# Weight steps put behind the float32 heads' exponentials, the first 24 feed-forward units ordered block by block, and other buffers for w_out

## The chip, the cores and the metric

The kernel runs on one core of one Trainium2 chip. The metric is the device time of one execution in microseconds (us). Matrix products run on the tensor engine (PE, its weight loads as PEld), activations and copies with a scale on the scalar engine (ACT), element-wise work on the vector engine (DVE), masks and reductions across partitions on GpSimd (POOL); the sync engine (SP) issues most DMAs, ACT those of the weights. Every engine takes its own queue in order.

## The reference

All inputs are float64. Attention over 8 batches of 8 heads with 576 positions and 64 channels, with a causal mask and a bias from a running sum of a gate `s`, is followed by a gated feed-forward layer over all 4608 tokens (512 channels, 1536 hidden).

```python
scores = scale * np.matmul(q, k.transpose(0, 1, 3, 2))
cum = np.cumsum(np.maximum(s, 0.0), axis=-1)
bias = -(cum[:, :, :, None] - cum[:, :, None, :])
scores = np.where(causal, -1000000000.0, scores + np.minimum(bias, 0.0))
attn = np.exp(scores - scores.max(-1, keepdims=True)); attn /= attn.sum(-1, keepdims=True) + 1e-09
x = np.matmul(attn, v).transpose(0, 2, 1, 3).reshape(B * S, H * D)
return ((1.0 / (1.0 + np.exp(-(x @ w_gate)))) * (x @ w_val) @ w_out).astype(np.float32)
```

## The kernel before

Operands are split into a high and a low float16 part, and three products of parts stand for one exact product. There are four kinds of work.

**Float32 heads.** Heads 0 to 7 (batch 0) are computed with float32 matmuls, tile by tile (five row tiles a head): scores on PE (L575), mask on POOL (L461), bias and row minimum on DVE (L584, tile `em`), exponential on ACT (L587), transposes on PE (L596), copies on ACT (L597), products with v on PE (L605).

**Float16 heads.** Heads 8 to 63 use the split operands (scores L446 and L447, minimum L471, exponential L474, splits L478, L483, L491, DMA transposes, products L506 to L511).

**Weight steps.** The weights arrive as 64-bit floats and are decoded on the chip. There are 18 steps (`wsteps`): steps 0 to 11 hold one block of 128 hidden columns of w_gate and w_val, steps 12 to 17 two such blocks of w_out. A step loads 1 MB in two DMAs issued by ACT (L253, L260), then runs as a chain across engines: ACT L272 (128x1024), DVE L273, L274, L275, ACT L287 (sum of squares), POOL L289, DVE L125 and L127 (a power of two as scale), ACT L292 (high part), DVE L293 (low part). Its raw words lie in a "room": `raw0`, or a quarter of the not yet written `w2all`, or a part of `t2big`, which later holds results of the first 24 units. Decoded words lie in `dec0` (tile `wa`) or in `w2all`; all six w_out steps use `dec0`, one after the other. `room(n)` also gives the step that must be through before the load of step n may be issued.

**Feed-forward units.** A unit (g, f) is 256 tokens times one block f of the hidden columns: 24 matmuls for gate and value (`ffn_in`, L657, tile `gv`), tanh on ACT (L662), the product on DVE (L664, tile `t2`). Then the two halves of h are made (`ffn_mid`, ACT L672 and DVE L673), and w_out is applied (`ffn_out`, L687, tile `o`, 6 matmuls with 512 columns). The scale of h (`hidden_scale`, tile `hsc`) needs the scales of all 18 weight steps. So the 24 units of the first two token groups (g = 0 and 1), whose x is ready after head 7, keep their t2 in `t2big` until step 17 is through; from g = 2 on, h follows at once.

The program is written as ticks, five to a head, and a list scheduler reorders the instructions of each engine when the kernel is built, by its own estimate of when each is ready; `tc.high_priority` and `tc.keep_in_program_order` constrain it, and the queue of each engine is then fixed. Weight steps are written at ticks below 44 (`min(2 + n // 8, 6)`: six of them) and, from tick 44 on, ahead of the units that need them: before unit 0, 3, 6, 9 the next three blocks, before unit 8 the first w_out step, from unit 12 all the others. Loads of steps 12 and 13 are written at ticks 22 and 30.

Of the kernel before, what the change touches and what calls it, by code (L numbers as in the profile page):

```python
# [23 lines left out]
def tile_attention_then_gated_ffn(  # L24
# [198 lines left out]
    for i in (1, 2):  # L223
        raw.append(t2big[:, 8 * i * GT : 8 * (i + 1) * GT].bitcast(I32).rearrange("p (n t) -> p n t", t=2))
    outroom = [(4, 0, 0), (5, 0, 0), (0, 0, NF - 3), (3, 0, NF - 1), (5, 0, NF + 1), (0, 0, NF + 2)]
# [9 lines left out]
    def load_weight(n):  # L235
# [3 lines left out]
        for x, src in enumerate((w_out,) if o else (w_gate, w_val)):  # L239
# [6 lines left out]
            if o == 0:  # L246
                src = src.rearrange("(c p) n -> p c n", p=P)
                dst = dst.rearrange("p (c x n) -> p c x n", c=NC, x=2)[:, :, x]
            else:

                src = src.rearrange("(x p) (h n) -> x p h n", p=P, h=8)
                dst = dst.rearrange("p (h x n) -> x p h n", x=2, h=8)
                ins = nc.scalar.dma_start(dst[0], src[0])  # L253
                if n < NF + 2:
                    tc.keep_in_program_order(ins)
                src, dst = src[1], dst[1]
            if n < 2:
                nc.sync.dma_start(dst, src)
            else:
                ins = nc.scalar.dma_start(dst, src)  # L260
                if n == 2 or NF <= n < NF + 2:
                    tc.keep_in_program_order(ins)

    def decode_weight(n):
# [7 lines left out]
        nc.scalar.activation(a.bitcast(F32), r[:, :, 1].bitcast(F32), AF.Copy, scale=2.0 ** -112)  # L272
# [45 lines left out]
    wnext = {"load": 0, "step": 0}  # L318

    def weight_step():  # L320
        n = wnext["step"]
        while n and wnext["load"] < len(wsteps) and room(wnext["load"])[2] < n:
            if not NF <= wnext["load"] < NF + 2:
                load_weight(wnext["load"])
# [253 lines left out]
    def n_max(i, t):  # L578
# [8 lines left out]
        nc.scalar.activation(e_t[t][:m, :w], e_t[t][:m, :w], AF.Exp, bias=init, scale=-1.0)  # L587
# [60 lines left out]
    def ffn_in(g, f):  # L648
# [14 lines left out]
        t2 = t2first[g * NF + f] if g < 2 else fp.tile([P, GT], F32, tag="t2", name=f"t2_{g}_{f}")  # L663
# [46 lines left out]
    units = [(g, f) for g in range(NG) for f in range(NF)]  # L710
# [9 lines left out]
    def emit_out():  # L720
        if state["o"] < len(units):
            ffn_out(*units[state["o"]])
# [15 lines left out]
    OUT = (22, 30)  # L738
    WLA = 3
    nticks = NTL * NH  # L740
    for n in range(nticks + 12):
# [43 lines left out]
        if i < NH:  # L785
# [96 lines left out]
            if n in OUT:  # L882
                load_weight(NF + OUT.index(n))
# [36 lines left out]
    for tt in range(GT // P):  # L920
        for u in range(state["o"], len(units)):
            ffn_out(*units[u], tiles=(tt,), last=True)
# [28 lines left out]
```

## Time and profile before

| | |
|---|---|
| time, median of 3 runs | 1153.24 us (1152.33 to 1156.69) |
| span of the profiled execution | 1146.4 us; its own time is not listed apart, the three runs are 5.9 to 10.3 us above the span |
| PE, busy | 1091.6 us (95%) |
| DVE, ACT, POOL, busy | 776.1, 749.5, 261.3 us |
| granted tensor clock, mean | 0.985 |
| the float32 heads | until 111.6 us (last exponential of head 7) |
| last weight step (low part, L293) | starts at 182.4 us |
| first w_out matmul | 189.0 us |

The span divides in two. From about 267 us on PE is busy nearly without a break. Ahead of that, float32 heads, weight steps, float16 heads 8 to 17 and the first 24 units share the engines, and PE waits now and then. Busy time counts overlapping instructions once. A matmul's record is longer than its pitch (a w_out matmul: record 0.379 us, one every 0.216 us), so a busy PE can be less than full.

### The profile page before, as it was taken

The numbers are of one execution on the slowest core, as the hardware profiler recorded it, in microseconds if no ns is written. First come the engines' busy times: TensorE is split into PE (matmuls) and PEld (weight loads), VectorE is DVE, ScalarE is ACT, GpSimd is POOL, SyncE is SP. The second block draws the span as 40 slices with busy tenths as digits, with TensorE's granted clock in tenths as the row PEclk, the third lists the DMA queues.
The fourth block names the chain that finished last, engine by engine and source line by source line (L and its number), as shares of the span: only waits on it lengthen the run. The fifth ranks groups of instructions, "written<-read, shape, count | busy, mean of one in ns | idle before, by whom it ended". The sixth has DMA issues, their size and how long they took to land.

```text
span 1146.4 us, 30336 instructions
## 1 busy us (share of the span) xinstructions
PE 1091.6 (95%) x11644; PEld 853.5 (74%) x11644; DVE 776.1 (68%) x2395; ACT 749.5 (65%) x1465; POOL 261.3 (23%) x568
## 2 busy tenths in 40 slices
PE   6787888989999999999999999999999999999998
PEld 4566676658767887788777777778877887787775
DVE  6899999866787777776565677777777775222222
ACT  6989778667777777676665577767776764233222
POOL 6634233222232222121211122212222221000000
PEclk9889899999999999999999999999999999999999
DMA  9676868995989888777646498868887774000000
GB/s 280 201 217 161 185 139 181 183 189 130 171 164 175 164 178 167 141 150 138 145 79 139 89 178 166 166 144 171 156 161 138 150 124 88 13 20 20 1 19 19
DMA packets 445518, 157.62 MB, mean 137 GB/s; under 512 B 403583, under 2 KB 435839, under 8 KB 445374
## 3 DMA queue, kind: packets, MB, share of 16 engines
q1 hardware_dynamic: 418686, 127.38, 57.6%
q10 hardware_dynamic: 23328, 17.04, 4.9%
q0 software_dynamic: 3360, 11.27, 3.0%
q8 instruction: 91, 1.49, 0.5%
q14 instruction: 53, 0.43, 0.1%
HBM read 56.92 MB, written 9.58 MB: 58 GB/s over the span
## 4 chain that ended last, share of the span: by engine, by line
PE 76%; DMA 7%; DVE 5%; issue 5%; ACT 5%; SPq 1%; POOL 1%; ACTq 0%; DVEq 0%; POOLq 0%
PE gv L657 42%; PE o L687 22%; PE s L447 3%; PE s L446 3%; DMA qk<-in_q_dram 1%; PE av L506 1%; PE av L508 1%; PE av L507 1%; DMA v<-in_v_dram 1%; DVE e L471 1%; PE s L575 1%; DMA pt<-p 1%; DMA T<-T 1%; PE na_ps L605 1%; DMA nqk<-in_q_dram 1%
## 5 line engine op out<-in xcount | busy, mean ns | idle before, releaser
L657 PE MATMUL gv<-x,w 128*128 128x256 f16 (+3 forms) x6912 | 613.2, 246 | 5.3 <-DVE t2f L664 2.7
L657 PEld LDWEIGHTS <-w 128*128 128x128 f16 x6912 | 533.8, 98 | 61.5 <-issue 5.2
L687 PE MATMUL o<-w2all,h 128*128 128x512 f16 x1296 | 314.8, 379 | 0.0
L461 POOL TENSOR_SCALAR_AFFINE_SELECT rl<-rl 128x64 f32<-128x64 f32 (+1 forms) x280 | 111.5, 399 | 519.7 <-DVE em L471 465.3
L474 ACT ACTIVATE e<-e,em 128x576 f32<-128x576 f32 x280 | 154.6, 554 | 92.3 <-DVE em L471 90.2
L687 PEld LDWEIGHTS <-h 128*128 128x128 f16 x1296 | 123.6, 98 | 108.7 <-issue 2.4
L662 ACT ACTIVATE th<-gv,scb 128x256 f32<-128x256 f32 (+3 forms) x288 | 111.4, 412 | 139.3 <-PE gv L657 138.4
L664 DVE SCALAR_TENSOR_TENSOR t<-th,gv 128x256 f32<-128x256 f32 x192 | 80.2, 417 | 133.5 <-ACT th L662 132.5
L471 DVE CUSTOM_DVE_ANT_0 e<-s,rl,qkcf 128x288 f32<-128x288 f32 x280 | 135.8, 485 | 30.5 <-PE s L447 24.9
L672 ACT ACTIVATE h<-t,hsc 128x256 f16<-128x256 f32 x192 | 96.6, 503 | 80.0 <-DVE t L664 80.0
L483 DVE SCALAR_TENSOR_TENSOR p<-e,p 128x384 f16<-128x384 f32 x224 | 102.0, 495 | 40.2 <-ACT p L478 39.4
L673 DVE SCALAR_TENSOR_TENSOR h<-t,hsc,h 128x256 f16<-128x256 f32 x192 | 93.2, 486 | 43.3 <-ACT h L672 42.8
L478 ACT ACTIVATE p<-e 128x1152 f16<-128x1152 f32 x112 | 112.1, 1001 | 2.8
L506 PE MATMUL av<-v,pt 128*128 128x65 f16 x560 | 68.0, 193 | 6.9 <-DMA pt<-p 6.9
L507 PE MATMUL av<-v,pt 128*128 128x64 f16 x560 | 68.0, 192 | 0.0
L446 PE MATMUL s<-T 128*128 128x288 f16 (+2 forms) x246 | 64.6, 280 | 3.6 <-DMA T<-qk 2.6
L508 PE MATMUL av<-v,pt 128*128 128x65 f16 x560 | 67.9, 194 | 0.0
L447 PE MATMUL s<-T 128*128 128x288 f16 (+2 forms) x246 | 62.2, 282 | 2.4 <-DMA T<-T 2.4
L506 PEld LDWEIGHTS <-pt 128*128 128x128 f16 x560 | 52.4, 97 | 13.6 <-DMA pt<-p 8.8
L706 POOL DMA_DIRECT2D out_dram<-osb x34 | 19.4, 570 | 174.6 <-ACT osb L705 173.8
L409 POOL PARTITION_BROADCAST cr<-cr x63 | 57.5, 913 | 6.1 <-DVE em L584 5.7
L455 DVE TENSOR_SCALAR rl<-cr,qkcf 128x576 f32<-128x576 f32 x56 | 29.1, 520 | 40.1 <-POOL cr L409 39.9
(157 smaller groups left out, 1436.9 us busy)
## 6 DMA issues: line engine op xcount, KB each, us to landing
v<-v SPq DMA_DIRECT2D x56, 162.5 KB
out_dram<-osb POOLq DMA_DIRECT2D x34, 256.0 KB, 2.9
v<-in_v_dram SPq DMA_DIRECT2D x64, 128.0 KB
T<-T SPq DMA_DIRECT2D x82, 72.0 KB
t2f<-in_v_dram SPq DMA_DIRECT2D x20, 288.0 KB
qk<-in_q_dram SPq DMA_DIRECT2D x17, 288.0 KB
qk<-in_k_dram SPq DMA_DIRECT2D x17, 288.0 KB
w2all<-in_moe_w_gate_dram ACTq DMA_DIRECT2D x7, 512.0 KB
```

What stands on the lines that cost most here:

```text
L446: nc.tensor.matmul(ps[:, : b_ - a], lhs, T[i][:, 0, a:b_], start=True, stop=False)
L447: nc.tensor.matmul(ps[:, : b_ - a], lhs, T[i][:, 2, a:b_], start=False, stop=True)
L461: nc.gpsimd.affine_select(rl[i][:, q0:w], rl[i][:, q0:w], pattern=[[-1, m]], compare_op=ALU.is_ge, fill=-MASKED if i < NN else MASKED, bas ...
L471: nc.vector.tensor_tensor_reduce(e_t[t][:, a:b_], ps[:, : b_ - a], rl[i][:, a:b_], c, init, ALU.add, ALU.min, acc)
L474: nc.scalar.activation(e_t[t][:, :w], e_t[t][:, :w], AF.Exp, bias=init, scale=-1.0)
L478: nc.scalar.activation(p_s[h_][:, 0], e_s[h_], AF.Copy, scale=PSCALE)
L483: nc.vector.scalar_tensor_tensor(flat[:, LOW[t] * P : (LOW[t] + t) * P], e_t[t][:, : t * P], PSCALE, flat[:, kb * P : (kb + t) * P], ALU.m ...
L506: nc.tensor.matmul(AV[i][:, t], hi, v_[:, D : 2 * D + 1], start=kb == 0, stop=False)
L657: nc.tensor.matmul(ps[:, gv, a:e], w1[f][:, cc, gv, wl], x_of(b, cc)[:, xl, c0 + a : c0 + e], start=(c == 0), stop=(c == 3 * NC - 1))
L662: nc.scalar.activation(th[:, a:e], ps[:, 0, a:e], AF.Tanh, scale=scb[b][:, f : f + 1])
L672: nc.scalar.activation(h[:, 0], t2, AF.Copy, scale=hsc[:, f : f + 1])
L687: nc.tensor.matmul(ps[:m], h[:, hl, tt * P : tt * P + m], w2[f][:, wl], start=(f == 0 and c == 0), stop=(f == NF - 1 and c == 2))
```

## The change

Four edits. The decode's first instruction (L272) is queued on ACT behind the exponential of a float32 head that was written last (`tc.issue_after`; it sets the order and waits for nothing). Seven steps in place of six are written below tick 44. The first 24 units are written block by block, (0,0), (1,0), (0,1), (1,1) and so on, in place of group by group, and the steps from 7 on are tied to blocks: three ahead each third block, step 12 from block 8 on, steps 13 to 17 at block 11. And the rooms of w_out change: only step 12 keeps a part of `t2big` as early room, the others reuse `raw0` and `w2all` once earlier steps have left them, so that loads 13 to 15 may be issued after step 11, load 16 after step 14, load 17 after step 16.

```diff
-    for i in (1, 2):
-        raw.append(t2big[:, 8 * i * GT : 8 * (i + 1) * GT].bitcast(I32)...)
-    outroom = [(4, 0, 0), (5, 0, 0), (0, 0, NF - 3), (3, 0, NF - 1), (5, 0, NF + 1), (0, 0, NF + 2)]
+    raw.append(t2big[:, 16 * GT : 24 * GT].bitcast(I32)...)
+    outroom = [(4, 0, 0), (2, 0, NF - 1), (0, 0, NF - 3), (3, 0, NF - 1), (0, 0, NF + 2), (0, 0, NF + 4)]
...
-        nc.scalar.activation(a.bitcast(F32), r[:, :, 1].bitcast(F32), AF.Copy, scale=2.0 ** -112)
+        with tc.issue_after(nexp["ins"].ins) if nexp["ins"] is not None else ExitStack():
+            nc.scalar.activation(a.bitcast(F32), r[:, :, 1].bitcast(F32), AF.Copy, scale=2.0 ** -112)
...
-        nc.scalar.activation(e_t[t][:m, :w], e_t[t][:m, :w], AF.Exp, bias=init, scale=-1.0)
+        nexp["ins"] = nc.scalar.activation(e_t[t][:m, :w], e_t[t][:m, :w], AF.Exp, bias=init, scale=-1.0)
...
-        t2 = t2first[g * NF + f] if g < 2 else fp.tile([P, GT], F32, tag="t2", name=f"t2_{g}_{f}")
+        t2 = t2first[2 * f + g] if g < 2 else fp.tile([P, GT], F32, tag="t2", name=f"t2_{g}_{f}")
...
-    units = [(g, f) for g in range(NG) for f in range(NF)]
+    outs = [(g, f) for g in range(NG) for f in range(NF)]
+    units = [(g, f) for f in range(NF) for g in range(2)] + outs[2 * NF :]
...
-    OUT = (22, 30)
+    OUT = 30
...
-            while n < NE and wnext["step"] < min(2 + n // 8, 6):
+            while n < NE and wnext["step"] < min(2 + n // 8, 7):
                 weight_step()
...
-                f = state["u"]
-                if f < NF and f % WLA == 0:
+                f, g = divmod(state["u"], 2)
+                if g == 0 and f % WLA == 0:
...
-                while f == 8 and wnext["step"] < NF + 1:
-                    weight_step()
-                while f >= NF and wnext["step"] < min(f + NF + WLA, len(wsteps)):
+                while f >= 8 and wnext["step"] < (NF + 1 if f < NF - 1 else len(wsteps)):
                     weight_step()
```

The scheduler turns this into other queues. Three places follow, where line numbers of the changed kernel are one higher for L587, L597 and L631 (588, 598, 632) and for L471, L483, L491, L474, L478, L662, L673 (472, 484, 492, 475, 479, 663, 674), and one lower for L253 and L260 (252, 259).

The first is ACT's queue at head 4, the float32 head in the middle. In a name like `em4_4_1` the first number is the head and the second the tile (tile 4 comes first); `w1_6` is the block of step 6. Before:

```order
L287 ACTIVATE w1_6_72,wss6_1566<-wa0_137 128x8x128
L260 DMA ws0_136<-in_moe_w_gate_dram 128x4x256
L260 DMA ws0_136<-in_moe_w_val_dram 128x4x256
L287 ACTIVATE w1_7_73,wss7_1581<-w2all_78 128x8x128
L260 DMA w2all_78<-in_moe_w_gate_dram 128x4x256
L292 ACTIVATE w1_5_71<-w2all_78,wscale_111 128x8x128
L260 DMA w2all_78<-in_moe_w_val_dram 128x4x256
L292 ACTIVATE w1_6_72<-wa0_137,wscale_111 128x8x128
L292 ACTIVATE w1_7_73<-w2all_78,wscale_111 128x8x128
L587 ACTIVATE e_1_80<-e_1_80,em4_4_1_739 128x576
L272 ACTIVATE w2all_78<-w2all_78 128x1024
L272 ACTIVATE wa0_137<-ws0_136 128x1024
```

The same place after:

```order
L598 COPY p16_0_81<-nt_ps_3_0_0_729 128x384
L292 ACTIVATE w1_3_69<-wa0_137,wscale_111 128x8x128
L588 ACTIVATE e_1_80<-e_1_80,em4_4_1_739 128x576
L588 ACTIVATE e_1_80<-e_1_80,em4_3_0_763 128x448
L588 ACTIVATE e_0_79<-e_0_79,em4_2_0_801 128x320
L598 COPY p16_1_82<-nt_ps_4_4_6_755 128x384
L598 COPY p16_1_82<-nt_ps_4_3_3_788 128x384
L588 ACTIVATE e_0_79<-e_0_79,em4_1_0_814 128x192
L272 ACTIVATE w2all_78<-w2all_78 128x1024
```

Steps 5, 6 and 7 stood ahead of head 4's first exponential; now step 3 does, and step 4 begins behind four of head 4's exponentials. By head 7's last exponential ACT had 14 instructions of L272 and 13 of L287 and L292 behind it; now it has 6 of each. On DVE 13 of L273, L274, L275 and L293 stood ahead of head 7's last row minimum; now 6, 6, 6 and 5.

The second place is DVE's queue at the first h (`h0_0`, the low half for unit (0,0)), the end of the wait for `hsc`. Before:

```order
L471 ISA em12_0_0_2975 128x1
L369 TENSOR_TENSOR qke7_2956<-expo_103,qk1_7_2954 128x2
L518 RECIPROCAL er11_3048<-er11_3048 128x5
L371 TENSOR_SCALAR qksc7_2958<-qke7_2956 128x2
L521 TENSOR_TENSOR xq5_2905<-av11_3007,er11_3048 128x5x64
L373 SCALAR_TENSOR_TENSOR qkcf7_2960<-qksc7_2958 128x1
L483 SCALAR_TENSOR_TENSOR p16_1_82<-e_1_80,p16_1_82 128x384
L483 SCALAR_TENSOR_TENSOR p16_1_82<-e_1_80,p16_1_82 128x512
L491 SCALAR_TENSOR_TENSOR p16_1_82<-e_1_80,p16_1_82 128x2x64
L374 SCALAR_TENSOR_TENSOR qkcf7_2960<-qksc7_2958 128x1
L673 SCALAR_TENSOR_TENSOR h0_0_2388<-t2f_135,hsc_112,h0_0_2388 128x256
```

After:

```order
L308 RECIPROCAL hsr_2383<-gmax_113 128x1
L316 TENSOR_SCALAR osc0_2386<-gmax_113,vin0_328 128x1
L316 TENSOR_SCALAR osc1_3132<-gmax_113,vin1_1004 128x1
L472 ISA e_0_79,em17_0_0_3748<-s17_0_0_3728,rl17_3549,qkcf8_3254 128x64
L472 ISA em17_0_0_3748 128x1
L309 TENSOR_SCALAR hsc_112<-hsg_2378,hsr_2383 128x12
L674 SCALAR_TENSOR_TENSOR h0_0_2388<-t2f_135,hsc_112,h0_0_2388 128x256
```

The first h stood behind head 12's row minima and now stands behind head 17's, 145 rows further down (row 437 before, 582 after), with all 24 units' t2 ahead of it, where there had been 14.

The third place is ACT's queue at the last load of w_out, that of step 17. Before, the load is issued here, 46 rows ahead of the L272 that reads it:

```order
L287 ACTIVATE w2all_78,wss14_1886<-wa0_137 128x1024
L253 DMA ws0_136<-in_moe_w_out_dram 128x8x128
L474 ACTIVATE e_1_80<-e_1_80,em9_4_1_1557 128x576
L260 DMA ws0_136<-in_moe_w_out_dram 128x8x128
L662 ACTIVATE th0_0_1374<-gv0_0_1349,scb0_1347 128x256
```

After, from the issue to the L272 that reads it:

```order
L252 DMA ws0_136<-in_moe_w_out_dram 128x8x128
L663 ACTIVATE th1_10_2249<-gv1_10_2224,scb0_1360 128x256
L259 DMA ws0_136<-in_moe_w_out_dram 128x8x128
L475 ACTIVATE e_0_79<-e_0_79,em15_2_0_3387 128x320
L475 ACTIVATE e_0_79<-e_0_79,em15_1_0_3396 128x192
L292 ACTIVATE w2all_78<-wa0_137,wscale_111 128x1024
L475 ACTIVATE e_0_79<-e_0_79,em15_0_0_3410 128x64
L663 ACTIVATE th0_11_2346<-gv0_11_2321,scb0_1360 128x256
L475 ACTIVATE e_1_80<-e_1_80,em16_4_1_3443 128x576
L479 ACTIVATE p16_0_81<-e_0_79 128x768
L272 ACTIVATE wa0_137<-ws0_136 128x1024
```

Seven compute instructions lie between the issue of the second half and the wait for it, and head 16's other exponentials are queued behind that wait. From unit (2,2) on, the queues of PE, ACT and DVE hold the same instructions in both kernels, in the same order but for a few neighbours that changed places.

More of the change, by code (lines that the diff above doesn't have):

```diff
@@ L322, in weight_step @@
         while n and wnext["load"] < len(wsteps) and room(wnext["load"])[2] < n:
-            if not NF <= wnext["load"] < NF + 2:
+            if wnext["load"] != NF:
                 load_weight(wnext["load"])
@@ L720, in emit_out @@
     def emit_out():
-        if state["o"] < len(units):
-            ffn_out(*units[state["o"]])
+        if state["o"] < len(outs):
+            ffn_out(*outs[state["o"]])
             state["o"] += 1
@@ L921, in tile_attention_then_gated_ffn @@
         for u in range(state["o"], len(units)):
-            ffn_out(*units[u], tiles=(tt,), last=True)
+            ffn_out(*outs[u], tiles=(tt,), last=True)
 _INS = ["q", "k", "v", "s", "moe_w_gate", "moe_w_val", "moe_w_out"]
```

11 lines of the change are left out of this document (6 added, 5 removed).

## The prediction

> **What bounds the kernel now.** I read the times, then busy time by stretch, then the groups of instructions, the timeline around the places where an engine stands, and last the queues. This view has, for each stretch of the span in us, the busy time of PE, PEld, DVE, ACT and POOL (count of instructions in brackets), the granted tensor clock, the DMA share and GB/s.
>
> ```profile
> 0.00:111.60 111.60, 83.46 (x484) 63.90 (x485) 93.91 (x241) 96.86 (x184) 58.58 (x109) 0.90 0.77 217
> 20.20:111.60 91.40, 71.98 (x446) 56.71 (x445) 80.03 (x209) 86.23 (x166) 47.42 (x75) 0.89 0.73 209
> 111.60:182.00 70.40, 59.24 (x576) 49.79 (x577) 62.77 (x174) 51.71 (x91) 20.91 (x38) 0.92 0.80 164
> 120.00:210.00 90.00, 77.49 (x803) 61.91 (x801) 82.46 (x256) 72.25 (x133) 30.39 (x55) 0.98 0.85 175
> 150.00:180.00 30.00, 24.21 (x273) 20.47 (x271) 28.88 (x83) 22.74 (x40) 12.03 (x20) 1.00 0.77 158
> 182.00:267.00 85.00, 78.43 (x774) 55.52 (x772) 65.90 (x224) 62.94 (x124) 24.75 (x49) 1.00 0.86 173
> 0.00:267.00 267.00, 221.13 (x1831) 169.22 (x1832) 222.57 (x637) 211.50 (x396) 104.23 (x196) 0.94 0.81 189
> 267.00:1146.00 879.00, 870.47 (x9820) 684.33 (x9816) 553.56 (x1759) 538.03 (x1070) 157.06 (x373) 1.00 0.62 122
> ```
>
> From 267 us on PE is the bound (870.5 of 879 us). Ahead of it stand three stages. In stage 1, the float32 heads (from 20.2, the end of head 0's last exponential, to 111.6, that of head 7's), ACT is the fullest, 86.2 of 91.4 us, which is 94%, and DVE has 88%. In stage 2, up to the last weight step, it is DVE with 62.8 of 70.4 us (89%). In stage 3, with w_out products as filler, PE has 92%.
>
> The change alters the queues only up to unit (2,2), which begins in this trace with this row of the timeline (start, us, engine, line and tiles; in brackets, where there is one, the wait before it and who ended it), behind the products of head 16. Behind it all queues hold the same work.
>
> ```profile
> 266.88 1.34 PE L657 MATMUL gv<-x,w 128*128 128x64 f16 x22
> ```
>
> So I ask one thing: when does the changed kernel reach 266.9?
>
> **Step 1, what leaves stage 1.** Here are the groups of a weight step (busy us, mean ns), from the groups by line of 0 to 267 us (a form with 8 or 6 of the 18 steps stands for all; idle time before them at the end).
>
> ```profile
> L272 ACT ACTIVATE w2all<-w2all 128x1024 f32<-128x1024 f32 x8 | 9.3, 1164 | 1.7 <-DMA w2all<-in_moe_w_val_dram 1.6
> L287 ACT ACTIVATE w<-w2all 128x1024 f16<-128x1024 f32 x8 | 8.5, 1057 | 1.3 <-DVE vsc L127 1.1 <-DVE vso L175 0.2
> L292 ACT ACTIVATE w<-w2all,wscale 128x1024 f16<-128x1024 f32 x8 | 9.1, 1137 | 0.0
> L273 DVE TENSOR_SCALAR w<-w2all 128x1024 int32<-128x1024 int32 x8 | 5.5, 693 | 2.2 <-ACT w2all L272 2.2
> L274 DVE SCALAR_TENSOR_TENSOR wa<-wa,w2all 128x1024 int32<-128x1024 int32 x6 | 7.3, 1212 | 0.0
> L275 DVE SCALAR_TENSOR_TENSOR wa<-ws,wa 128x1024 int32<-128x1024 int32 x6 | 7.4, 1226 | 0.0
> L293 DVE SCALAR_TENSOR_TENSOR w<-w2all,wscale,w 128x1024 f16<-128x1024 f32 x8 | 10.2, 1276 | 1.0 <-ACT w L292 1.0
> L125 DVE TENSOR_SCALAR xe_w<-wtot 128x1 int32<-128x1 int32 x18 | 2.6, 146 | 6.4 <-POOL wtot L289 6.3
> L127 DVE TENSOR_SCALAR wscale<-xe_w 128x1 int32<-128x1 int32 (+1 forms) x18 | 3.3, 186 | 0.2
> L289 POOL PARTITION_ALL_REDUCE wtot<-wss x18 | 9.2, 512 | 37.2 <-ACT w2all L287 28.3 <-ACT w L287 8.7
> ```
>
> By the queues, ACT loses from stage 1 eight L272 (1.16) and seven each of L287 (1.06) and L292 (1.14): 24.7 us, about 23 once 0.1 us of overlap each is taken off. Some splits of float16 head 9 move ahead, 1 to 2 us. That leaves 86.2 - 21.5 = 64.7 us on ACT. DVE loses seven each of L273, L274, L275 (3.13 together), eight L293 (10.2) and seven pairs of small ones (2.3): 34.4, some 31 after overlap, so it keeps 93.9 - 31 = 63 from the start and 49 in the stage. POOL loses seven reductions of 0.5. The two DMA issues of each step are on ACT's queue too, but its sequencer issues them beside compute: in the rows that follow, an issue of 0.86 us at 130.72 lies over computing from 130.41 to 131.35, and the next instruction starts at 131.45 without a wait. So they cost nothing while ACT has work at hand, and at most 14 times 0.5 to 0.9 us otherwise.
>
> ```profile
> 130.41 1.05 ACT L287 ACTIVATE w2all<-wa 128x1024 f16<-128x1024 f32 x1
> 130.72 0.86 ACTq L260 DMA_DIRECT2D ws<-in_moe_w_out_dram  x1
> 131.35 0.20 ACT L287 ACTIVATION_READ_ACCUMULATOR w2all<-wa 128x1 f32 x1
> 131.45 0.77 ACT L474 ACTIVATE e<-e,em 128x576 f32<-128x576 f32 x1
> ```
>
> PE's work in stage 1 stays, but 27 us of the first 119 ran at half clock, the first 17 of them in the pile-up of steps 5 to 7 ahead of head 4, whose last minimum on DVE came 30 us after head 3's:
>
> ```profile
> 49.31 0.22 DVE L584 CUSTOM_DVE_ANT_0 e<-s,cr 64x64 f32<-64x64 f32 x1
> 79.56 0.21 DVE L584 CUSTOM_DVE_ANT_0 e<-s,cr 64x64 f32<-64x64 f32 x1
> 50.14 0.41 PE L629 MATMUL nx_ps<-ident,nx 128*128 128x128 f32 x2 [2.96 <-DVE x L632]
> 51.00:68.00 17.00, 13.33 (x54) 11.15 (x53) 13.36 (x32) 15.86 (x31) 5.74 (x8) 0.51 0.58 167
> 109.00:119.00 10.00, 9.50 (x48) 8.14 (x47) 7.01 (x15) 6.18 (x13) 1.33 (x2) 0.52 0.65 149
> ```
>
> At full clock PE's 72 us would be about 64 (half of the 13.3 and of some 2.5 us). So ACT with 64.7 and PE with 64 are level. If ACT runs without a gap, stage 1 ends at 20.2 + 64.7 = 85 us; at the 94% of before at 89; if PE sets it at the 79% of before, at 101. Two engines that are level and feed each other run a little below the 94%: I take 91 us, nearest to ACT's row. **Saved in stage 1: 20.6 us** (bounds 10 and 27).
>
> **Step 2, what comes into stage 2.** Before unit (2,2) DVE has the same 222.6 us in both kernels. In the changed queue 63 come up to head 7's last minimum, and behind the first h come the 24 halves of h and little else:
>
> ```profile
> L673 DVE SCALAR_TENSOR_TENSOR h<-t2f,hsc,h x24: 467/478/692, 187.4 to 257.8; 128x256 f16<-128x256 f32 x24
> ```
>
> 24 times 0.48 less overlap is 10, and rows of some ten other kinds, counted in the queue by the means of their groups, add 10.5. So 222.6 - 63 - 20.5 = 139 us of DVE work stand between, heads 8 to 17 and twelve weight steps together, and ACT has some 115 there. All of it has to go before the first h, since DVE takes its queue in order, where before heads 13 to 17 came behind. How full DVE runs there decides the case. At the 89% of 111.6 to 182 it takes 156 us, at the 91.6% of 120 to 210 it takes 152, at the 96% of the best 30 us 144, and without a gap 139. I take 92%, 151 us, the nearest row a little rounded up, because weight work stands ready over the whole stage. PE, with 24 units and ten float16 heads, has 89 us of work there and waits.
>
> The last load of w_out is one more wait in this stage. The first loads show the latency, issue at 4.19 and a waiting ACT until 10.31:
>
> ```profile
> 4.19 0.51 SPq L258 DMA_DIRECT2D ws<-in_moe_w_val_dram  x1
> 10.31 1.15 ACT L272 ACTIVATE wa<-ws 128x1024 f32<-128x1024 f32 x1 [1.85 <-DMA ws<-in_moe_w_val_dram]
> ```
>
> Against these 6.1 us stand seven instructions on ACT: four exponentials (0.56 each), a tanh (0.45), L292 (1.14) and an L478 on 768 columns (0.8 of the 1.0 of its mean), 4.6 us, about 4.2 less overlap.
>
> ```profile
> L474 ACT ACTIVATE e<-e,em 128x576 f32<-128x576 f32 (+4 forms) x52 | 28.8, 558 | 7.4 <-DVE em L471 7.2
> L662 ACT ACTIVATE th<-gv,scb 128x256 f32<-128x256 f32 (+2 forms) x28 | 12.3, 445 | 3.6 <-PE gv L657 3.4
> L478 ACT ACTIVATE p<-e 128x1152 f16<-128x1152 f32 (+1 forms) x20 | 20.0, 998 | 0.3
> ```
>
> Head 16's exponentials wait behind L272, and DVE's splits behind those. Bounds are 0, if those seven wait for DVE anyway, and 5, if the load meets the transposes (DMA share 0.86 there); I take 2. The other loads of w_out have 14 or more compute rows of cover and cost nothing, unless DMA falls behind by more than 10 us. The first h comes at 91 + 151 + 2 = 244 us, against 187.4.
>
> **Step 3, what is left for PE.** Behind the first h the changed queue of PE holds all 144 w_out matmuls, half of units (2,0) and (2,1) and the products of heads 15 and 16. A w_out matmul comes every 0.216 us:
>
> ```profile
> 254.07 4.48 PE L687 MATMUL o<-w2all,h 128*128 128x512 f16 x20
> L687 PE MATMUL o<-w2all,h x144: 377/379/380, 189.0 to 262.3; 128*128 128x512 f16 x144
> ```
>
> That is 144 x 0.216 = 31.1, and 6.3 for the rest (54 gate matmuls, mostly 0.08 and 0.03, and 80 head products at 0.03). 37.4 us with DVE and ACT at half load, plus 1 us of gaps: 38.4. Before, part of these had filled gaps from 189 us on. Unit (2,2) is reached at 244 + 38.4 = 282.4, against 266.9: 15.5 us later. PE's waits behind that point may shrink, as DVE is ahead by then; they are 2.7, 0.4 and 1.4 us in the three stretches below, 4.5 in all, of which I take 3.5.
>
> ```profile
> 270.00:300.00 30.00, 27.31 (x415) 22.67 (x414) 20.22 (x68) 20.49 (x47) 4.49 (x12) 1.00 0.84 163
> 300.00:330.00 30.00, 29.58 (x367) 23.58 (x365) 23.94 (x78) 22.33 (x46) 8.72 (x20) 1.00 0.88 164
> 330.00:360.00 30.00, 28.61 (x282) 21.60 (x281) 26.67 (x93) 24.65 (x46) 8.81 (x19) 1.00 0.87 178
> ```
>
> **Edits with no price of their own.** The block order makes ACT, DVE and PE do the same 24 units; it lets a unit pair wait for one block where three were needed, and its effect is inside step 2. The index of `t2big` follows it. Step 12's room, units 16 to 23, is read by L275 well ahead of unit (0,8) in DVE's queue. Seven POOL reductions move past the heads' masks into a stage where POOL has 20.9 of 70.4 us. SP issues the same DMAs, the heads' ones earlier. The 7 MB of loads that come later meet a DMA share of 0.80; if that cover is gone, it shows as DVE waiting, and is in step 2's 89% end.
>
> **The sum.** -20.6 in stage 1; stages 2 and 3 then last 191.4 us from 91 to 282.4, where they lasted 155.3: +36.1; -3.5 behind. That is +12 us on a span of 1146.4. The runs' median is 6.8 above the span, so 1153.2 + 12 = **1165 us**, slower by 1.0%.
>
> **Rivals.** *Faster.* The pile-up was dearer than its parts: without it ACT runs through stage 1 in 85 us with PE at full clock, and DVE, never short of weight work, runs stage 2 at 98% or more (142 us, load 17 hidden): first h at 227, unit (2,2) at 264, and 4.5 behind: -7, 1146 us. It decides once the first h comes before some 227 us. For it speaks the 0.51 clock from 51 to 68; against it that no stretch above has DVE over 96%. Chance 0.08.
>
> *The same.* Stage 1 in 89, DVE at the 96% of 150 to 180: 89 + 144 + 37.5 = 270.5, +3.6, less 3.5: 1153 to 1157 us. Needs five times that stretch in a row. Chance 0.20.
>
> *The clock falls in stage 2.* PE has 89 us of work in 151, so it waits more. The rows above show half clock after a wait of 2.96 us, and full clock again 17 us later. If a third of stage 2 ran at half clock, its score and unit matmuls double: PE has room for it, but each of about three heads gets some 2.7 us longer from scores to minimum, +8 us: 1173 us. Against it: from 150 to 180 the clock was 1.00 though PE was busy for 24.2 of 30 us, its gaps short. Chance 0.12. The Trainium skill ("TensorE: Matmul & The Clock Gate", Part 1) says that the tensor clock is halved after an idle window of about 3.4 us and comes back after a busy one as long. By that rule short waits as from 150 to 180 leave it full, and this rival would need waits of the length seen at 50.14; the trace agrees so far, with 0.51 behind a wait of 2.96.
>
> *It does less than it says.* Seven steps are written among the heads, but by the queues six are through when head 7 ends, against 13; were seven or eight through in effect, 5 to 9 us of DVE work would stay in stage 1, and the end would move by less than that, into the case above. No chance of its own.
>
> **Numbers.** My own forecast, slower by 6 to 28 us without a lower clock, has 0.60. Within it and the clock's case the time is over 1159; "the same" is 0.5% (5.8 us) on each side, about what a measurement of this kernel can tell from no change. So faster 0.08, same 0.20, slower 0.72. The range reaches from 1148, where most of the faster case is left out, to 1180: stage 1 at 95, DVE at the 89% end (156) and the load's 5 us give +27 before the 3.5, and the clock's case lies inside.
>
> **What the profile will show.** Right: head 7's last exponential (L588) near 91 us; 13 of the 18 low parts (L293) behind it; the first h (L674) near 244 us with DVE at about 92% from 91 on and PE below 70% full; then w_out matmuls almost back to back; unit (2,2) near 282. Wrong in step 1, if head 7 ends past 97 or before 86; in step 2, if the first h comes before 235; in step 3, if unit (2,2) comes less than 35 us behind the first h. The forecast falls if DVE has over 96% throughout stage 2, or if something other than DVE, such as the chain of the six w_out steps through the single `wa`, holds the first h past 255.

## The result, and the profile after

The changed kernel takes 1184.11 us (median of four runs, 1179.94 to 1191.05), against 1153.0 for the kernel before: a ratio of 1.0271, 95% interval 1.0228 to 1.0313. It is 31 us slower, where 12 were forecast, and outside the range. A second series of the same kernel gave 1182.97 us and 1.0267 (1.0238 to 1.0296).

The profile shown here is of the slowest of the four runs (1191.05 us). The second series gave one of 1185.33 us, which is read beside it. The profile of before errs the other way: the profiled times of the runs below are 1.7 to 2.1 us above their spans, so its span of 1146.4 us belongs to an execution of some 1148.3 us, 5 below the median. Differences between the traces are larger by these amounts than those between the medians.

First the busy time by stretch, as in the prediction: of the changed kernel its three stages and the rest, then all up to unit (2,2); the last row is that of the kernel before for the same work.

```profile
20.20:106.00 85.80, 72.40 (x445) 59.94 (x444) 51.80 (x164) 64.58 (x138) 34.90 (x68) 0.83 0.54 151
106.00:266.90 160.90, 110.06 (x1047) 87.91 (x1046) 137.28 (x390) 115.15 (x194) 59.43 (x84) 0.83 0.84 167
266.90:307.50 40.60, 40.23 (x293) 21.65 (x293) 22.45 (x57) 23.81 (x48) 5.07 (x11) 0.95 0.62 146
307.50:1189.00 881.50, 872.18 (x9824) 685.73 (x9820) 551.88 (x1755) 536.78 (x1068) 157.51 (x371) 1.00 0.62 121
20.20:307.50 287.30, 222.70 (x1782) 169.50 (x1781) 211.53 (x609) 203.53 (x378) 99.40 (x163) 0.85 0.72 159
```

```profile
20.20:266.90 246.70, 209.55 (x1789) 161.92 (x1788) 208.59 (x605) 200.78 (x378) 92.97 (x162) 0.94 0.80 184
```

The bounds of the stages are these starts of groups (head 7's last exponential is the last of L588, the first h the first of L674) and of unit (2,2) on PE:

```profile
L588 ACT ACTIVATE e<-e,em x40: 333/562/797, 11.1 to 106.0; 128x576 f32<-128x576 f32 x8, 128x448 f32<-128x448 f32 x8, 128x320 f32<-128x320 f32 x8, 128x192 f32<-128x192 f32 x8
L674 DVE SCALAR_TENSOR_TENSOR h<-t2f,hsc,h x24: 473/483/508, 266.9 to 300.9; 128x256 f16<-128x256 f32 x24
307.52 2.84 PE L658 MATMUL gv<-x,w 128*128 128x64 f16 x48
```

Unit (2,2) begins 40.6 us later than before, and PE's account tells of what kind these are. Its matmuls are the same, yet it is busy for 222.7 us instead of 209.6: 13.1 us more, at a granted clock of 0.85 instead of 0.94. And it stands for 64.6 instead of 37.2 us: 27.4 more. What it waited for shows in the waits (us in all, times, longest), of the changed kernel and then of the one before, both from 100 to 267 us:

```profile
PE s L447 <- DVE em L472: 17.5, 10, 3.6
PE s L447 <- DMA T<-qk: 15.4, 3, 6.5
PE av L507 <- DMA pt<-p: 11.5, 6, 3.7
```

```profile
PE av L506 <- DMA pt<-p: 6.9, 7, 2.2
PE s L446 <- DMA T<-qk: 2.6, 3, 1.1
PE s L446 <- DVE em L471: 0.6, 1, 0.6
```

Two kinds of wait have grown: PE waits for transposes by DMA (26.9 us in these rows, 9.5 before), and for row minima, which free the banks its scores go to (17.5 against 0.6).

### The profile page after: what moved, and what is told of

Its sections match the earlier page's. It is cut to its first block, busy times and chain, and to the rows that moved or that the text cites. A ratio compares the mean times of both kernels' runs of the same rounds, so it can differ in the third digit from the quotient of the medians.

```text
span 1189.1 us, 30359 instructions
## 1 busy us (share of the span) xinstructions
PE 1107.4 (93%) x11644; PEld 864.2 (73%) x11644; DVE 777.3 (65%) x2395; ACT 751.3 (63%) x1465; POOL 268.1 (23%) x568
## 4 chain that ended last, share of the span: by engine, by line
PE 73%; DMA 5%; DVE 4%; ACT 2%; issue 2%; SPq 1%; POOL 1%; DVEq 0%; ACTq 0%; POOLq 0%
PE gv L658 41%; PE o L688 22%; DMA pt<-p 3%; PE s L448 3%; PE s L447 3%; PE av L507 1%; PE av L509 1%; PE av L508 1%; DVE p L484 1%; DMA v<-in_v_dram 1%; DVE e L472 1%; PE av L511 1%; PE av L512 1%; POOL rl L462 0%; DMA qk<-in_q_dram 0%
## 5 line engine op out<-in xcount | busy, mean ns | idle before, releaser
L462 POOL TENSOR_SCALAR_AFFINE_SELECT rl<-rl 128x64 f32<-128x64 f32 (+1 forms) x280 | 125.5, 449 | 546.3 <-DVE em L472 482.4
L673 ACT ACTIVATE h<-t,hsc 128x256 f16<-128x256 f32 x192 | 96.7, 503 | 82.4 <-DVE t L665 81.5
L674 DVE SCALAR_TENSOR_TENSOR h<-t,hsc,h 128x256 f16<-128x256 f32 x192 | 93.2, 485 | 43.9 <-ACT h L673 43.6
L447 PE MATMUL s<-T 128*128 128x288 f16 (+2 forms) x246 | 66.9, 290 | 33.6 <-DVE em L472 18.1
L448 PE MATMUL s<-T 128*128 128x288 f16 (+2 forms) x246 | 64.6, 289 | 4.5 <-DMA T<-T 4.5
L507 PEld LDWEIGHTS <-pt 128*128 128x128 f16 x560 | 52.7, 98 | 19.9 <-DMA pt<-p 13.1
L508 PEld LDWEIGHTS <-pt 128*128 128x128 f16 x560 | 52.9, 98 | 4.7
```

The lines of the kernel that those rows point to most:

```text
L447: nc.tensor.matmul(ps[:, : b_ - a], lhs, T[i][:, 0, a:b_], start=True, stop=False)
L448: nc.tensor.matmul(ps[:, : b_ - a], lhs, T[i][:, 2, a:b_], start=False, stop=True)
L462: nc.gpsimd.affine_select(rl[i][:, q0:w], rl[i][:, q0:w], pattern=[[-1, m]], compare_op=ALU.is_ge, fill=-MASKED if i < NN else MASKED, bas ...
L507: nc.tensor.matmul(AV[i][:, t], hi, v_[:, D : 2 * D + 1], start=kb == 0, stop=False)
L508: nc.tensor.matmul(AV[i][:, t, 0:D], hi, v_[:, 0:D], start=False, stop=False)
```

## The experiments

Times are compared by ratios to the kernel before in the same series; "over before" is the ratio less one, times 1153 us. The changed kernel stands at +31. For thin loads, filled waits and shortened work, the program was built as always and single instructions were then exchanged, added or left out in the finished queues, so that all others keep their places.

### Which edit costs what

`e1_issue_only` is the kernel before with `tc.issue_after` alone. `e3_blocks_only` has the other edits, without it and without the seventh step. `e4_six` is the changed kernel with one edit undone:

```diff
-            while n < NE and wnext["step"] < min(2 + n // 8, 7):
+            while n < NE and wnext["step"] < min(2 + n // 8, 6):
```

> The kernel before with the first edit alone: L272 is queued behind the float32 head's exponential that was written last. Six steps below tick 44, the group order of the first 24 units and the old rooms of w_out stay. By the queues this alone takes the weight steps out of stage 1 (6 of 18 L292 ahead of head 7's last exponential, as with all edits, against 13 before), and the first h stands behind head 15 on DVE, against head 12 before and head 17 with all edits. Theory A, the first edit carries the loss: 1170 to 1185 us, head 7's last exponential near 106 us, tensor clock under 0.9 on average up to the first h. Theory B, the block order and the late w_out loads carry it: 1150 to 1162 us. My forecast's view (weight work is only moved, DVE stays full) would give 1158 to 1168.

> The changed kernel without its first two edits: block order of the first 24 units, steps tied to blocks and the new rooms of w_out, but L272 free to run ahead among the float32 heads, and six steps below tick 44. By the queues 13 of 18 L293 stand ahead of head 7's last row minimum, as before, and the first h behind head 14. Theory A (the first edit carries the loss): 1150 to 1160 us. Theory B (block order and late loads carry it): 1170 to 1185 us, with head 7's end near 112 us as before and the first h later than 200 us.

> The changed kernel with six steps below tick 44 in place of seven; all other edits stay. By the queues only some neighbours change places, and the first h stands behind the same rows. All theories: the seventh step is worth nothing by itself, 1180 to 1188 us, within 4 us of the changed kernel's 1184.

> The changed kernel itself once more, on the same chip as the two others: a second profile of it, since the first fell on the slowest of its four runs (1191.05 us). 1179 to 1188 us; head 7's last exponential at 101 to 106 us, the first h at 255 to 267 us, 80 to 106 us at half clock.

| | us | ratio (95%) | over before |
|---|---|---|---|
| e1_issue_only | 1171.18 | 1.0155 (1.0107 to 1.0203) | +18 |
| e3_blocks_only | 1166.85 | 1.0116 (1.0073 to 1.0159) | +13 |
| e4_six | 1183.06 | 1.0279 (1.0238 to 1.0319) | +32 |
| after_again | 1182.97 | 1.0267 (1.0238 to 1.0296) | +31 |

Neither theory A nor B holds alone: the two halves cost 18 and 13 us, and together they make the 31. With the first edit alone head 7's last exponential comes at 101.1 us and the first h at 246.3; with the other edits alone they come at 116.3 and 214.0. The seventh step is worth nothing, as expected. The second profile of the changed kernel has head 7's last exponential at 101.6, the first h at 263.2 and unit (2,2) at 303.6 us.

### The bytes of the late loads

Weight DMAs from step 7 on move 16 partitions by one piece, with the waits and semaphores of the DMA in whose place they stand. Those of step 12, and with the old rooms of step 13 too, stay whole. The diff says it in short:

```diff
-ACT: dma_start(o, s)                    # 512 KB
+ACT: dma_start(o[:16, :1], s[:16, :1])  # 16 KB for w_gate and w_val, 8 KB for w_out
```

> The changed kernel with every queue as it is, but the weight loads of steps 7 to 11 and 13 to 17 move 16 partitions by one piece instead of 128 by four or eight, about 1/32 of their bytes; those steps decode old words, so the numbers that come out are other ones. Same instructions on every engine. Theory E, weight loads that now fall into stage 2 hold up the transposes of heads 8 to 17 (the chain of waits goes through a transpose of 11.7 us at 147 and one of 8.2 us at 164), and these hold up everything: 10 us or more are won, 1174 us or less, first h at 255 or earlier. Theory A or D (order of the queues, not bytes): 1179 to 1187 us, first h within 5 us of 267.

> A control for thin_after: the kernel before, its queues kept, with the same thin weight loads from step 7 on (step 12's and 13's, into unused room, stay; the output is another one). Theory E, it is the loads that the change moved to 116 to 164 us that hold up the transposes: before they went out by 131 us and cost little, so 1148 to 1154 us. Rival: the bytes of the weights cost the same wherever they lie: 1138 to 1145 us.

> e1_issue_only (first edit alone, 1171.2 us) with thin weight loads from step 7 on, queues kept, the two early w_out loads whole (the output is another one). Here w_out keeps the rooms of before, so fewer loads lie late. Theory E (bytes of late loads hold up the transposes): the first edit alone also makes the gate and value loads late, 4 to 9 us won, 1162 to 1167 us. Rival: the first edit costs by order alone, 1169 to 1173 us.

> e3_blocks_only (block order and new rooms alone, 1166.9 us) with thin weight loads from step 7 on, queues kept (the output is another one). Theory E: the w_out loads that the new rooms delay are what the edit costs, 6 to 13 us won, 1154 to 1161 us. Rival: it costs because the first h comes behind all 24 units, 1163 to 1168 us.

| thin loads in | us | ratio (95%) | over before | whole loads |
|---|---|---|---|---|
| changed kernel | 1170.68 | 1.0149 (1.0113 to 1.0184) | +17 | +31 |
| kernel before | 1150.76 | 0.9990 (0.9971 to 1.0010) | -1 | 0 |
| e1_issue_only | 1166.12 | 1.0134 (1.0091 to 1.0177) | +15 | +18 |
| e3_blocks_only | 1152.97 | 1.0021 (0.9999 to 1.0044) | +2 | +13 |

This is the clearest result. Nearly the same bytes (9 MB thinned there, 10 here) cost nothing measurable in the kernel before, some 14 us in the changed one (give or take 6, by the two intervals), and nearly all of what the block order and the new rooms cost. Where they hurt is seen in the changed kernel's chain of waits (start, us, what), in ACT's DMA issues and in SP's issues of the transposes that feed head 9's and 10's products:

```profile
147.18 11.65 DMA pt<-p
164.19 8.24 DMA pt<-p
```

```profile
143.78 0.57 ACTq L252 DMA_DIRECT2D ws<-in_moe_w_out_dram  x1
144.38 1.19 ACTq L259 DMA_DIRECT2D ws<-in_moe_w_out_dram  x1
150.38 0.55 ACTq L252 DMA_DIRECT2D w2all<-in_moe_w_out_dram  x1
151.00 0.65 ACTq L259 DMA_DIRECT2D w2all<-in_moe_w_out_dram  x1
163.62 0.55 ACTq L252 DMA_DIRECT2D w2all<-in_moe_w_out_dram  x1
164.24 0.65 ACTq L259 DMA_DIRECT2D w2all<-in_moe_w_out_dram  x1
```

```profile
147.18 4.55 SPq L495 DMA_TRANSPOSE pt<-p  x1
164.19 3.65 SPq L495 DMA_TRANSPOSE pt<-p  x1
171.64 1.56 SPq L495 DMA_TRANSPOSE pt<-p  x1
```

A transpose behind a pair of w_out loads took 11.65 and 8.24 us from issue to use (one of 12.09 in the second profile); with thin loads no transpose of `p` stands in this chain before 261 us. In stage 1 it is the same: step 8's loads went out at 94.62 and 95.25, head 8's transpose of q and k at 95.1, and PE, ACT and DVE all stood behind its landing:

```profile
94.62 0.39 ACTq L259 DMA_DIRECT2D w2all<-in_moe_w_gate_dram  x1
95.25 0.53 ACTq L259 DMA_DIRECT2D w2all<-in_moe_w_val_dram  x1
104.68 1.03 PE L447 MATMUL s<-T 128*128 128x288 f16 x3 [6.46 <-DMA T<-qk]
```

With thin loads the same transpose was issued at 95.15, and PE waited 0.71 us for it:

```profile
98.66 0.68 PE L447 MATMUL s<-T 128*128 128x288 f16 x2 [0.71 <-DMA T<-qk]
```

In the kernel before, the last weight load went out at 130.7 us, and the transposes of `p` had just begun (this row merges two, issued at 127.54 and 132.20):

```profile
127.54 6.49 SPq L494 DMA_TRANSPOSE pt<-p  x2
```

So the two hardly met there; one transpose of q and k, issued at 108.39 behind w_out loads at 106.63 and 107.32, took 5.67 us to its use. Theory E holds: the bytes of the late loads cost the time. That they cost it through the transposes is read from the chain. Standing among transposes isn't enough either: with the first edit alone, four w_out loads also go out between 131 and 188 us, and there thin loads won only 3 us by the ratios, 5 by the medians, which is within the noise.

Stage 2 with thin loads, and the waits left in it:

```profile
101.50:249.30 147.80, 105.73 (x1035) 83.67 (x1035) 136.79 (x389) 114.62 (x194) 57.95 (x84) 0.84 0.66 125
```

```profile
PE s L447 <- DVE em L472: 19.8, 12, 3.7
PE s L447 <- DMA T<-qk: 6.7, 2, 6.3
PE av L507 <- DMA pt<-p: 4.6, 4, 2.0
```

DVE now has 136.8 of 147.8 us, 92.6%, about the share that the forecast had taken.

### The tensor clock

Transposes of the identity matrix were put on PE ahead of its longest waits, into a bank that nobody else used at that point:

```diff
+PE: transpose(spare_bank, ident, ident)   # n times, about 75% of the wait
 PE: the matmul that waits
```

> The changed kernel with every queue as it is, but 349 transposes of the identity matrix on PE, which nobody reads, put ahead of the 28 matmuls that PE waited longest for up to 267 us (some 75% of each wait at 0.11 us a transpose; 18 of them in the float32 heads, the others from 112 us on). They fill waits and so hold the tensor clock up. Theory C, the lower clock in stage 2 is itself a cause (106 us at half clock up to 343 us, against 34 before): 8 us or more are won, 1176 us or less, the first h at 255 or earlier. Theory D, the clock fell only because PE had to wait, and PE is off the path there: 1180 to 1190 us, the clock of stage 2 above 0.95 all the same and the first h within 4 us of 267; a little slower still if the transposes are in the way.

> The two edits of w_after and thin_after together on the changed kernel's queues: thin weight loads from step 7 on (without step 12's; the output is another one) and 305 unread transposes on PE in the 28 longest waits left in the thin kernel's trace. Theory F, low clock and transposes held up by loads are two separate causes: the gains of 7.5 us and 13.4 us add, 1160 to 1165 us, which is where my forecast lay; stage 2 at DVE 92% or more, first h at 243 or earlier. Rival G, both took away the same waits: 1167 to 1172 us, no better than the thin loads alone.

> The kernel before with its queues, and 162 unread transposes on PE ahead of the 27 matmuls it waited longest for up to 180 us (some 75% of each wait; 10 more ahead of one in head 4): a control for w_after, and a candidate that might beat both kernels. 31 us ran at half clock between 20 and 130 us. Theory C (a low clock is a cause wherever PE or what it feeds is on the path): 2 to 8 us won, 1146 to 1151 us, half-clock time under 15 us. Rival D: 1152 to 1156 us, the transposes only fill waits.

> w_before (kernel before with 162 unread transposes, 1148.3 us) with 46 more of them ahead of the waits that were left at 57, 110 and 115 us, after which its tensor clock still fell for 13.7 and 6.8 us. If a low clock in the float32 heads costs where PE feeds the others, another 1 to 4 us are won, 1144 to 1148 us, and the half-clock time after 20 us goes from 20.5 to under 8 us. If PE's waits there are only ends of round trips, 1147 to 1151 us, no better than w_before.

| filled waits in | us | ratio (95%) | over before | not filled |
|---|---|---|---|---|
| changed kernel | 1176.62 | 1.0205 (1.0164 to 1.0247) | +24 | +31 |
| changed, thin loads | 1167.30 | 1.0142 (1.0128 to 1.0156) | +16 | +17 |
| before (162) | 1148.32 | 0.9971 (0.9956 to 0.9986) | -3 | 0 |
| before (208) | 1152.38 | 0.9994 (0.9977 to 1.0010) | -1 | 0 |

The number in brackets is that of the added transposes. Stages 1 and 2 of the changed kernel with filled waits, then with thin loads too:

```profile
20.20:99.70 79.50, 69.59 (x466) 57.98 (x465) 52.12 (x164) 64.79 (x139) 35.72 (x68) 0.89 0.58 167
99.70:256.20 156.50, 137.90 (x1376) 121.43 (x1375) 137.00 (x389) 115.22 (x194) 58.93 (x84) 0.96 0.84 172
```

```profile
20.20:99.40 79.20, 71.73 (x493) 59.30 (x491) 52.21 (x166) 64.80 (x140) 34.14 (x68) 0.94 0.51 142
99.40:248.70 149.30, 125.66 (x1308) 108.31 (x1308) 136.89 (x389) 114.27 (x194) 58.51 (x84) 1.00 0.67 124
```

With whole loads the clock was a cause: with the waits filled it was 0.96 instead of 0.83 in stage 2, and 7.5 us came back, though the added transposes are extra work. That is half a microsecond short of what theory C named. Not all of it is stage 2's: this stage went from 160.9 us (161.6 in the second profile) to 156.5, and stage 1, where 18 of the added transposes stand, ended earlier too. With thin loads, a clock of 1.00 in stage 2 gave back only 1 to 3 us (1 by the ratio, 3.4 by the medians). So the causes don't add (rival G): the low clock follows the long waits, and makes what comes after them slower. Of the two tries on the kernel before, the first is faster by 0.3%, and so faster than both kernels; the second showed no difference, although its granted clock over its runs was the higher one (0.993 against 0.988 on average). The two profiles have the same 20.5 us at half clock behind 20 us, where under 8 were expected of the second. That a warm clock won the 0.3% is not shown, and I would not build on it.

### What sets the stages

`pv_after` and `pv_w_thin` leave out 48 of the float32 heads' 120 products with v. `d_w_thin` and `d_thin` let the decode work on 64 columns from the seventh step on. Again in short:

```diff
-PE: 15 products of a head's p and v
+PE: 9 of them (the inner ones of each sum are left out)
```

```diff
-DVE: L274, L275 on 128x1024
+DVE: L274, L275 on 128x64
```

> The changed kernel with its queues, less 48 of the float32 heads' 120 products with v (the inner ones of each sum, six a head, so the output is another one): 48 times 2 times 0.112, 10.8 us of PE at full clock out of 72 us in stage 1. Theory P, PE sets the end of stage 1 in the changed kernel: head 7's last exponential comes 6 to 12 us earlier, near 97 us (106.0 in the changed kernel, 99.7 to 101.5 in its variants), and the total falls by 4 to 10 us. Rival Q, the order on ACT and DVE or the transposes of head 8 set it: less than 3 us earlier. If the tensor clock falls more often because PE has less to do, the gain is under 6 us and the half-clock time in stage 1 over 30 us.

> w_thin (1167.3 us) with 48 of the float32 heads' 120 products with v left out as in pv_after, all queues kept (the output is another one). If PE is what still holds stage 1 (head 7's last exponential at 99.4, forecast 91), it ends 6 to 10 us earlier, at 90 to 93 us, and the total falls as far, 1157 to 1161 us. If the order on ACT and DVE or head 8's loads hold it, it ends past 96 us and the total stays over 1163 us.

> w_thin (changed kernel's queues, thin loads, transposes in the waits; 1167.3 us, first h at 248.7), and on top of that the decode's two DVE instructions L274 and L275 work on 64 of 1024 columns from the seventh step on (24 instructions, about 1.05 us less each, 25 us of DVE work taken out of stage 2; the output is another one). Theory R, DVE's in-order queue sets the first h, as the forecast had it: 18 us or more are won up to the first h (231 or earlier), and 10 to 18 us in total, PE being then the next bound. Rival S, stage 2 is a chain of round trips (scores, minima, exponentials, transposes) in which DVE only happens to be full: first h 240 or later, less than 8 us in total.

> thin_after (1170.7 us, first h at 249.3) with the two decode instructions L274 and L275 on 64 of 1024 columns from the seventh step on, 25 us less DVE work in stage 2, and without the added transposes that filled PE to 90% in d_w_thin (the output is another one). Theory R, DVE's in-order queue sets the first h: 18 us or more are won up to the first h, 231 or earlier, and 10 us or more in total, 1160 us or less. Theory S, a chain of round trips in which DVE is only one stage: first h 240 or later, 1162 us or more.

| | us | ratio (95%) | over before | without this edit |
|---|---|---|---|---|
| pv_after | 1172.03 | 1.0192 (1.0172 to 1.0212) | +22 | +31 |
| pv_w_thin | 1162.33 | 1.0084 (1.0057 to 1.0112) | +10 | +16 |
| d_w_thin | 1159.98 | 1.0071 (1.0041 to 1.0102) | +8 | +16 |
| d_thin | 1163.03 | 1.0100 (1.0061 to 1.0140) | +12 | +17 |

Here is stage 1 of `pv_after`, of `pv_w_thin`, of `thin_after` and of `d_thin`, and last stage 2 of `d_thin`.

```profile
20.20:94.70 74.50, 63.40 (x370) 50.06 (x369) 51.64 (x165) 64.43 (x139) 33.92 (x68) 0.87 0.60 175
```

```profile
20.20:96.00 75.80, 64.95 (x410) 51.04 (x408) 52.36 (x166) 64.44 (x139) 34.20 (x68) 0.91 0.53 150
```

```profile
20.20:101.50 81.30, 74.04 (x463) 61.31 (x462) 52.30 (x166) 64.74 (x138) 34.15 (x68) 0.85 0.50 138
20.20:94.20 74.00, 66.21 (x464) 54.63 (x463) 51.55 (x164) 64.27 (x139) 35.15 (x68) 0.95 0.54 152
```

```profile
94.20:232.90 138.70, 101.48 (x1034) 81.98 (x1034) 114.74 (x390) 113.31 (x194) 46.48 (x84) 0.87 0.70 133
```

PE does hold the kernel up in stage 1 (theory P): with 10.8 us less work for it (9.0 us less busy in this stage, against the first profile) the total falls by 9 us. Head 7 ends at 94.7 instead of 106.0 (101.6 in the second profile), but that alone would show little, since the end of this stage varies from one execution to the next. `d_thin` leaves PE all its work and has the same instructions as `thin_after` ahead of head 7's end, and yet stage 1 ended at 94.2 instead of 101.5, at a clock of 0.95 instead of 0.85. When clock and loads are out of the way too, leaving out the same products brings 5 to 7 us in total, and 99.4 to 96.0 at the end of the stage, against 90 to 93 expected. At the end no engine is over 86% there; that hand-over between engines is what remains is inferred from this, not shown.

In stage 2 theory R fails: the first h came at 232.9 us in `d_thin` and at 243.5 in `d_w_thin`, where 231 or earlier was named. Theory S fits `d_w_thin` (240 or later was named, and under 8 us in total; it was 7 by the medians, 8 by the ratios), and `d_thin` in the total but not in the first h. DVE is more than a bystander, though. Of some 25 us of DVE instructions (22 us of its busy time in stage 2), 9.1 come back in `d_thin` as a shorter stage (147.8 to 138.7); 7.3 more at the first h came from the earlier end of stage 1, in this one profile. In `d_w_thin` stage 2 won 6.0 (149.3 to 143.3), with a PE that the transposes filled. In total it is 6 to 8 us. DVE's queue is one limit of stage 2, worth a quarter to a third of what is taken from it, not the limit.

## Why the prediction was right or wrong

The sign was right (0.72 on slower), the size not: +31 by the medians where +12 was forecast. By its own steps, with the two profiles of the changed kernel:

| term | forecast | measured |
|---|---|---|
| end of stage 1 | 91 | 106.0; 101.6 |
| stage 2 with load 17 | 153 | 160.9; 161.6 |
| first h to unit (2,2) | 38.4 | 40.6; 40.4 |
| regained behind unit (2,2) | 3.5 | none: 2.0 longer; 0.2 longer |
| total, against the span of before | +12 | +42.7; +36.9 |

**Step 1 failed.** The work was summed rightly: ACT has 64.6 us where 64.7 was forecast, DVE 51.8 where 49. "Two engines that are level and feed each other run a little below the 94%" is the sentence that was wrong, twice. PE was put at full clock, 64 us, though the row ahead of it had 0.51; it ran at 0.83 and 0.90 and took 72.4 and 67.9 us. The prediction put that low clock down to the pile-up of steps 5 to 7. The pile-up is gone in the changed kernel, and the clock fell at the same place all the same:

```profile
49.20:52.60 3.40, 2.47 (x12) 2.10 (x12) 0.84 (x3) 3.35 (x10) 1.74 (x4) 0.50 0.44 126
52.60:62.80 10.20, 10.10 (x35) 8.31 (x35) 3.13 (x9) 3.61 (x7) 0.83 (x3) 0.50 0.43 119
```

In every one of the eighteen traces a stretch at half clock begins between 45 and 61 us. And the pair of engines, level by the forecast, did not run at 91%: ACT's share was 75 and 80%, 85% with PE relieved, loads thin and waits filled, and 87% at the most, in `d_thin`. No run of this queue reached 91 us; 94.2 is the earliest. The bound at PE's 79%, 101 us, stood in the text and was the better row.

**Step 2's sum was right, its share was not, because of one term.** 139 us of DVE work was forecast, 137.3 measured; PE was 68% busy, below the 70% named. DVE's share was 85%, below the 89% that the prediction kept for loads without cover; its 92% came true (92.6%) only with thin loads. By the prediction's own sign, something other than DVE held the first h past 255. The failed term is that the other loads of w_out "cost nothing, unless DMA falls behind by more than 10 us", with the 7 MB said to "meet a DMA share of 0.80". DMA did fall behind: one transpose took 11.65 us. And 0.80 is an average share, which says nothing of who stands behind a load. The transposes that feed PE do, and the loads moved from a stretch with hardly any transposes into one that lives on them. The term priced at nothing cost some 14 us, counted with the loads of steps 7 to 11, which were thinned along with it. The load that was priced, that of step 17 at 2 us, cost none: ACT's L272 waited 0.7 us, and for DVE.

**Step 3 was right** within 2.2 us, and w_out products ran almost back to back (40.23 of 40.60 us). The 3.5 us to be regained behind it were a guess at PE's waits; nothing was regained.

**The rivals.** The clock's case was priced at 8 us, and holding the clock up gave 7.5. Stage 2 was at half clock for a third of its time (0.83 granted), as that rival supposed. That the figures are so near is in part luck, since stage 2 by itself gave 4 to 5 us in the profiles and the rest came in stage 1, which the rival left out. Its chance of 0.12 was too low, since the waits that bring the clock down were taken from a stretch in which the loads were over. The faster rival asked for the first h before some 227; it came at 263 and 267.

**What stays open.** With thin loads and filled waits the changed order still costs 16 us, nearly all of it by the first edit (thin loads leave +15 there, +2 with the other edits). In that run's profile it comes from a stage 1 that shrinks by some 12 us instead of 20.6, while stage 2 gets the whole moved work. Which hand-overs hold stage 1 at 94 to 100 us, and why its end varies by several us, was not settled.

## What to carry to other kernels

When a change moves transfers, ask for each which other transfers and which waiting engine stand in its new stretch: nearly the same bytes cost nothing where they met hardly any DMA transposes, and with all edits some 14 us among them. Taking work off the fullest engine buys at most the distance to the next one, and that one must be counted at the clock and the share it really ran with. A busy sum tells how much must go through an engine, not that the engine sets the pace: here 22 us less busy time on an engine at 93% gave 6 to 8.

## What the runs showed of the hardware

**The clock fell without an idle window.** The clock's records change in pieces of 3.41 us. I cut all eighteen traces, from 20 to 270 us, into these pieces and took PE's busy share of each by the profile's records. Of 1038 at full clock, the next was at half clock in all 57 in which PE was busy for less than 40%, in 18 of 26 between 40 and 50%, in 27 of 104 between 50 and 70%, and in none of 851 with more. In 38 of the 102 falls PE's longest gap within the piece was under 1.5 us. One such fall, the piece ahead of it and the first behind it, and PE's rows in it:

```profile
73.10:76.50 3.40, 2.04 (x16) 1.39 (x15) 1.20 (x10) 3.34 (x9) 0.60 (x2) 1.00 1.00 334
76.50:79.90 3.40, 2.76 (x12) 2.09 (x10) 1.92 (x3) 2.10 (x5) 1.87 (x2) 0.50 1.15 329
```

```profile
73.94 0.55 PE L597 MATMUL nt_ps<-ident,e 128*128 128x128 f32 x3 [0.66 <-ACT p L598]
74.68 0.69 PE L559 MATMUL nq_ps<-ident,nqk 96*128 96x96 f32 x6 [0.19 <-PE nt_ps L597]
75.88 1.08 PE L597 MATMUL nt_ps<-ident,e 128*128 128x128 f32 x6 [0.51 <-ACT p L598]
```

PE was busy for 60% of the piece, its longest wait was 0.66 us, and half clock followed. The Trainium skill ("TensorE: Matmul & The Clock Gate", Part 1) asks for an idle window of some 3.4 us; by these traces a window that is half busy can be enough, and the prediction leaned on the stricter rule when it called short waits harmless. The wait of 2.96 us that it took as agreeing with the page is shorter than that window, too. The way back was slower than the one busy window that the page names, above all up to 112 us, where the float32 heads run: of 91 half-clock pieces there in which PE was busy for 80% or more, full clock followed on 41; of 62 behind 112 us, on 57.

**A transpose's issue can stretch behind loads.** In the changed kernel SP's issue of a transpose of `p` took 3.3 to 5.3 us in the four cases up to 260 us that lay within 3.1 us of a w_out load's second half, and 1.3 to 2.2 us otherwise; with thin loads it was 1.3 to 2.2 up to 260 us. Weight loads are neither needed for it nor always enough: in the kernel before, five took 3.0 to 4.1 us between 188 and 252 us, where no weights are loaded any more, and the one at 132.2 us, 1.5 us behind a w_out load's second half, took 1.8.
